# Attention and feed-forward kernel: order and form of the first transfers, z spread by TensorE products, scales of values and M from squares

## The chip, the cores and the metric

The kernel runs on one core of a Trainium2 chip. The metric is the device time of one execution in microseconds (us). A core has five engines that run their own instruction streams side by side: TensorE (PE: matrix products, results in PSUM), VectorE (DVE), ScalarE (ACT: functions and copies), GpSimd (POOL) and SyncE (SP, which here only issues transfers). Each takes its instructions strictly in order, and semaphores make one wait for another. 16 DMA engines move data. TensorE runs at one of two levels of its clock, 1.2 or 2.4 GHz; the profile shows the granted share.

## The reference

Four batches of 8 heads, 576 rows, head size 64. The heads' outputs are laid side by side and become 2304 rows of 512 for a two-layer network.

```python
scores = np.where(causal, -1e9, q @ k.T / sqrt(D));  a = softmax(scores)   # rows + 1e-9
local = a @ v
q_p = phi(q)                                   # phi(x) = x + 1 for x > 0, else exp(x)
mem_out = (q_p @ M_prev) / (q_p @ z_prev + 1e-6)
x = sigmoid(beta) * mem_out + (1 - sigmoid(beta)) * local     # -> 2304 x 512
h = x @ w_in                                   # 512 x 2048
g = np.maximum(h, 0) + alpha * np.minimum(h, 0)
out = g @ w_out                                # 2048 x 512
```

w_in and w_out lie in memory as 64-bit numbers; the kernel makes 32-bit numbers of them by integer operations on VectorE.

## The kernel before

**Stages.** The first 64 rows of all four batches (256 rows, called Z in the code) are done first, with `load_first`, `first_scores` and `first_values`. The remaining 512 rows of each batch follow, in units of a head, with scores, probabilities and values on TensorE, and each 256 rows that are ready go through the network (`moe_in`, `moe_out`) in steps of 256 columns of w_in. The network runs twice over the rows, once for each half of the 2048 columns. The first groups take the weights of the first half as 32-bit numbers; later groups take them as two 16-bit parts in three products.

**Weights.** A piece of w_in is 128x1024 numbers in two transfers of 512 KB (its two column halves). `load_w` loads it, `conv_w` makes 32-bit numbers by three VectorE operations on 128x1024 (`to_f32`) and lets ScalarE square it with a running sum, which gives the weights' scale. `split_w` makes the 16-bit parts. Four pieces form w_in's first half.

**Scales.** Values and M go into one matrix beside each other and need a power of two as scale. Before, VectorE finds their largest magnitude: `prep_vZ` (first rows, two reduces of 128x1024), `prep_v0` (batch 0, three reduces) and `prep_v` (batches 1 to 3, one of 128x2048 and one of 128x512 each). `powers` and `exponents` turn it into a power of two through a transpose and a product on TensorE. The scale stands ahead of the probabilities: their products with it on VectorE must be done before TensorE can transpose them and form the values.

**Other names.** `ones` is the operand of the warm-up products that TensorE does at the start (WARM, 66 before); R is the store of the weights, part of which holds first rows' data at the start; stv and mw hold the largest magnitudes, mv those of batch 0; P the probabilities, PT their transposes, s scores in PSUM, h and y the network's results in PSUM, x the rows that enter the network, gg the activated h; kn, q, vn, zb, E are loads' buffers.

**Order.** Every operation is first recorded by the class `Work`, then issued in the order of the table PLACES, which holds a place for each operation of each phase (so nearly every instruction has the same line in the profile, L827). The order on each engine, SP's included, is thus fixed by that table. It was found by a search with the prices in `price`. All loads of the kernel are issued by SP in one queue:

```python
at = [next(places[op[7]]) for op in self.ops]
for i in sorted(range(len(at)), key=at.__getitem__):
    _, fn, a, kw = self.ops[i][:4]
    fn(*a, **kw)
```

## Time and profile before

| | |
|---|---|
| runs | 544.98, 545.71, 549.67 us, median 545.71 |
| the profiled execution | 547.0 us |
| its span in the profile | 545.2 us |
| TensorE / VectorE / ScalarE / GpSimd busy | 96% / 83% / 69% / 12% |
| chain that ended last | PE 68%, DVE 17%, DMA 7%, ACT 3% |
| granted clock, mean | 0.99 |

An engine is busy when it executes an instruction; the share is an average over stages. The span runs from the first to the last instruction that the profile shows. The windows give busy time in stretches of the span, and the chain of waits follows back, from the last instruction, what released each step.

### The profile page before, as it was taken

The page shows a single profiled execution, that of the slowest core. Times are in us where ns is not written, and L with a number is a line of the kernel's source. Part 1 is how long each engine was busy: PE and PEld are TensorE (multiplying, and loading weights), DVE is VectorE, ACT ScalarE, POOL GpSimd, SP SyncE. Part 2 cuts the span into 40 slices and gives each one's busy share as a digit, 9 for nine tenths or more (in the row PEclk, how much of TensorE's full clock was granted, in tenths as well). Part 3 has the DMA queues.
Part 4 walks back from the last instruction along what each step waited for, and adds up shares of the span by engine and source line. Part 5 has one row for each costly group of instructions (what it writes and reads, how often), then busy time and mean ns, then how long its engine had stood idle before and what let it go on. Part 6 is the DMA issues. An engine that isn't in the chain of part 4 may idle for free.

```text
span 545.2 us, 11977 instructions
## 1 busy us (share of the span) xinstructions
PE 525.1 (96%) x4421; PEld 352.8 (65%) x4421; DVE 451.3 (83%) x1197; ACT 376.4 (69%) x790; POOL 65.1 (12%) x142
## 2 busy tenths in 40 slices
PE   8849999999998999999999999999999999999997
PEld 3537655756676666668576666667676667676663
DVE  5999999999999999999989999978798866533231
ACT  1659888688987578888779788786776755422322
POOL 3000420001110011111112111021211110000000
PEclk9969999999999999999999999999999999999999
DMA  8999968763599989669999826787725534401101
GB/s 289 216 336 205 266 173 226 214 128 95 135 157 185 222 211 176 143 149 179 208 205 229 187 60 129 165 185 160 135 50 112 107 88 117 88 21 49 38 1 38
DMA packets 226026, 82.84 MB, mean 152 GB/s; under 512 B 216224, under 2 KB 216240, under 8 KB 225968
## 3 DMA queue, kind: packets, MB, share of 16 engines
q1 hardware_dynamic: 225968, 82.09, 67.4%
q8 instruction: 34, 0.56, 0.4%
q14 instruction: 24, 0.20, 0.1%
HBM read 35.66 MB, written 5.77 MB: 76 GB/s over the span
## 4 chain that ended last, share of the span: by engine, by line
PE 68%; DVE 17%; DMA 7%; ACT 3%; issue 3%; SPq 2%; POOL 0%; DVEq 0%; ACTq 0%; POOLq 0%
PE h L827 28%; PE y L827 27%; PE s L827 6%; PE bank L827 5%; DMA PT<-P 3%; DVE R L827 3%; DVE E L827 2%; DVE P L827 2%; DVE gg L827 2%; DMA E<-in_moe_w_in_dram 2%; SPq L827 2%; DVE r L827 1%; ACT P L827 1%; DMA R<-in_M_prev_dram 1%; DMA R<-in_moe_w_in_dram 1%
## 5 line engine op out<-in xcount | busy, mean ns | idle before, releaser
L827 PE MATMUL y<-R,gg 128*128 128x512 f16 (+1 forms) x832 | 274.7, 397 | 0.0
L827 PE MATMUL h<-x,R 128*128 128x256 f16 x1536 | 267.3, 273 | 0.2
L827 PEld LDWEIGHTS <-R 128*128 128x128 f16 x1536 | 142.2, 98 | 47.5 <-issue 1.9
L827 PE MATMUL bank<-v,PT 128*128 128x64 f16 x1224 | 146.8, 193 | 3.2 <-DMA PT<-P 3.1
L827 PEld LDWEIGHTS <-PT 128*128 128x128 f16 x1224 | 97.7, 98 | 33.4 <-DMA PT<-P 4.1
L827 PEld LDWEIGHTS <-gg 128*128 128x128 f16 x768 | 73.5, 98 | 39.4 <-DVE gg L827 0.6
L827 ACT ACTIVATE E<-E,mx 128x192 f32<-128x192 f32 (+3 forms) x136 | 81.1, 600 | 25.6 <-DVE mx L827 22.1
L827 POOL TENSOR_SCALAR E<-q,nrm,sm 128x64 f32<-128x64 f32 x112 | 50.5, 463 | 337.2 <-DVE sm L827 263.3
L827 ACT ACTIVATE P<-E,mx 128x640 f16<-128x640 f32 (+3 forms) x112 | 71.8, 673 | 20.0 <-POOL E L827 10.1
L827 DVE SCALAR_TENSOR_TENSOR P<-E,mx,P 128x384 f16<-128x384 f32 (+3 forms) x112 | 76.2, 699 | 7.4 <-ACT P L827 6.0
L827 DVE SCALAR_TENSOR_TENSOR r<-r,oma,h 128x256 f32<-128x256 f32 x128 | 57.5, 475 | 24.2 <-ACT r L827 24.0
L827 ACT ACTIVATE r<-h 128x512 f32<-128x512 f32 x72 | 42.2, 589 | 32.7 <-PE h L827 28.2
L827 DVE SCALAR_TENSOR_TENSOR gg<-r,gsc,gg 128x512 f16<-128x512 f32 x56 | 41.8, 748 | 25.6 <-ACT gg L827 15.2
L827 DVE CUSTOM_DVE_ANT_0 E<-s,mask,pm 128x576 f32<-128x576 f32 (+3 forms) x96 | 57.3, 612 | 4.6 <-PE s L827 3.0
L827 ACT ACTIVATE gg<-r,gsc 128x512 f16<-128x512 f32 x56 | 40.0, 715 | 30.1 <-PE y L827 22.9
L827 PE MATMUL s<-k,qT 128*128 128x64 f16 (+5 forms) x136 | 36.4, 290 | 0.2 <-DVE mx L827 0.2
L827 PE MATMUL s<-k,qS 128*128 128x192 f16 (+4 forms) x120 | 34.8, 294 | 0.0
L827 PE MATMUL h<-R 128*128 128x256 f32 x128 | 32.1, 386 | 0.1
L827 PEld LDWEIGHTS h<-R 128*128 128x128 f32 x128 | 22.7, 190 | 5.6 <-issue 2.1
L827 ACT ACTIVATE xn<-bank,xsc 128x256 f16<-128x256 f32 x28 | 13.1, 469 | 15.3 <-PE bank L827 15.0
L827 ACT ACTIVATION_READ_ACCUMULATOR E<-E,mx 128x1 f32 x124 | 23.3, 188 | 0.0
L827 DVE SCALAR_TENSOR_TENSOR R<-R,wsc 128x1024 f16<-128x1024 f32 x16 | 20.5, 1280 | 0.1
(183 smaller groups left out, 618.1 us busy)
## 6 DMA issues: line engine op xcount, KB each, us to landing
q<-in_q_dram SPq DMA_DIRECT2D x16, 256.0 KB, 5.3
vn<-in_v_dram SPq DMA_DIRECT2D x16, 256.0 KB, 5.1
out_dram<-t SPq DMA_DIRECT2D x16, 256.0 KB, 2.4
kn<-in_moe_w_in_dram SPq DMA_DIRECT2D x6, 512.0 KB, 7.6
kn<-in_moe_w_out_dram SPq DMA_DIRECT2D x6, 512.0 KB, 5.8
kn<-in_k_dram SPq DMA_DIRECT2D x12, 256.0 KB, 3.8
qS<-qT SPq DMA_DIRECT2D x24, 128.0 KB, 2.7
R<-in_moe_w_in_dram SPq DMA_DIRECT2D x4, 512.0 KB, 5.7
```

The lines of the kernel that those rows point to most:

```text
L827: fn(*a, **kw)
```

## The change

**Transfers.** The first rows' loads now come ahead of most of the weights: of the four w_in pieces only the first column half is loaded and made into 32-bit numbers at first (`load_w` and `conv_w` with `cs=(0,)`), the second halves follow. The conversion of these four pieces is in operations of 128x512 in place of 128x1024. Values and M of the first rows come in four transfers of 64x16x64 in place of eight of 64x8x64. alpha, beta and z are issued by ScalarE, not SP.

**z.** z of the first rows, needed on 64 partitions for each batch, was loaded four times with the row repeated. Now four rows are loaded once (4x512), and two TensorE products with a 0/1 matrix spread them over the partitions; ScalarE copies the result from PSUM.

**Scales.** The reduces of `prep_vZ`, `prep_v0` and `prep_v` are gone. ScalarE squares the values (times 2^-10) and sums along each row, and the scale's exponent is taken from the largest of these sums, halved; constants are adapted (SQ, GS, 2^13).

**TensorE at the start.** Warm-up products go from 66 to 40, and two products of 128x256 follow on each of the four converted first halves (PACE) whose results nobody reads.

**Places.** Phases are finer (a name for each head, piece or step), the planner's prices are new, and PLACES is found anew.

```diff
-WARM = 16, 50
+WARM = 16, 24
+PACE = 2
...
     def load_first():
-        for b in range(B):
-            load(*zload(zb[ps, t], b), "Lz")
+        zr = R[12][0:B, 0:H * D]
+        A.dma_start(out=zr, in_=z_prev.rearrange("b h d -> b (h d)"))
...
-        for b in range(B):
-            vv = nat[Z]["v"][b // 2][:, b % 2]
-            Y.dma_start(out=vv[64:128], in_=v[b, :, 0:64, :].rearrange("h p d -> p h d"))
-            Y.dma_start(out=vv[0:64], in_=M_prev[b].rearrange("h d e -> d h e"))
+        for t in range(2):
+            for ps, src in ((slice(64, 128), v[2 * t:2 * t + 2, :, 0:64, :]), (slice(0, 64), M_prev[2 * t:2 * t + 2])):
+                Y.dma_start(out=nat[Z]["v"][t][ps].rearrange("p b h d -> p (b h) d"), in_=src.rearrange("b h p d -> p (b h) d"))
...
     def conv_w(s, cs=(0, 1)):
+        for c in (0, 512) if len(cs) == 1 or not WC[s] else (0,):
+            n = 512 if len(cs) == 1 or not WC[s] else 1024
...
+        if s < 4 and not cs[0]:
+            for i in range(PACE):
+                T.matmul(h0[:, 0], lhsT=r[:, 0:128], rhs=r[:, 0:256], start=True, stop=True)
...
     def prep_vZ():
         for i in range(2):
-            V.tensor_reduce(mv[:, i:i + 1], vn[i].rearrange("p t h d -> p (t h d)"), **ab)
+            A.activation(R[0], vn[i].rearrange("p t h d -> p (t h d)"), AF.Square, scale=2.0 ** -SQ, accum_out=mv[:, i:i + 1])
...
     def prep_v(b):
-        V.tensor_reduce(sv, vn[:, :, 1:NS].rearrange("p h i d -> p h (i d)"), **dict(ab, axis=AX.XY))
-        V.tensor_reduce(mv[:, 0:1], vn[:, :, 0], **dict(ab, axis=AX.XY))
+        A.activation(p["q16"][:, 0:2048].rearrange("p (h c) -> p h c", h=H), vn[:, :, 1:NS].rearrange("p h i d -> p h (i d)"),
+                     AF.Square, scale=2.0 ** -SQ, accum_out=sv)
+        A.activation(p["q16"][:, 0:512].rearrange("p (h c) -> p h c", h=H), vn[:, :, 0], AF.Square, scale=2.0 ** -SQ,
+                     accum_out=mv[:, 0:1])
...
+    zs = R[12][0:B, 512:768]
+    A.copy(zs.rearrange("p (b n) -> p b n", b=B), ident[0:B, 0:B][:, :, None].to_broadcast([B, B, 64]))
+    for t in range(2):
+        pt = psp.tile([128, 512], F32, tag="y", bufs=2)
+        T.matmul(pt, lhsT=zs[:, 128 * t:128 * t + 128], rhs=R[12][0:B, 0:H * D], start=True, stop=True)
+        A.copy(nat[Z]["z"][t].rearrange("p h d -> p (h d)"), pt)
...
     def weights(i):
-        load_w(8 * i)
-        for s in range(8 * i, 8 * i + 8):
+        if i == 0:
+            for f in (load_w, conv_w):
+                for c in range(2):
+                    for s in range(4):
+                        f(s, (c,))
+            w_scale(0)
+        first = 8 * i if i else 4
+        load_w(first)
+        for s in range(first, 8 * i + 8):
```

SP's queue before, from its first load of k on (64x8x64 is a first-row load of one batch; by here all eight w_in halves and q are issued):

```order
L827 DMA R<-in_k_dram 64x8x64 x3
L827 DMA q_1_94<-in_z_prev_dram 64x512
L827 DMA R<-in_k_dram 64x8x64
L827 DMA R<-in_v_dram 64x8x64 x2
L827 DMA R<-in_M_prev_dram 64x8x64 x2
L827 DMA R<-in_v_dram 64x8x64
L827 DMA R<-in_M_prev_dram 64x8x64
L827 DMA R<-in_v_dram 64x8x64
L827 DMA R<-in_M_prev_dram 64x8x64
L827 DMA q_2_95<-in_q_dram 128x8x64 x2
```

And SP's queue now, from its first instruction on:

```order
L1740 DMA R<-in_moe_w_in_dram 128x1024
L1740 DMA R<-in_k_dram 64x8x64
L1740 DMA q_0_93<-in_q_dram 64x8x64 x4
L1740 DMA R<-in_moe_w_in_dram 128x1024
L1740 DMA R<-in_k_dram 64x8x64 x2
L1740 DMA R<-in_M_prev_dram 64x16x64
L1740 DMA kn_90<-in_moe_w_in_dram 128x1024
L1740 DMA R<-in_k_dram 64x8x64
L1740 DMA R<-in_v_dram 64x16x64
L1740 DMA R<-in_M_prev_dram 64x16x64
L1740 DMA E_0_92<-in_moe_w_in_dram 128x1024
L1740 DMA R<-in_v_dram 64x16x64
```

The last first-row load is now behind four w_in halves (128x1024 of 32-bit words each) in place of eight, and no load of z stands among them.

VectorE's piece before at which the first rows' values and M are reduced, behind the maxima of the scores (ISA rows), up to the start of the scale:

```order
L827 TENSOR_REDUCE stv_137<-R 128x1 x2
L827 ISA P_100,zmx_134<-s_0_68,mz 128x64
L827 ISA zmx_134 128x1
L827 TENSOR_TENSOR stv_137<-stv_137 128x1
L827 TENSOR_REDUCE stq_85<-q_2_95 128x1
L827 SCALAR_TENSOR_TENSOR tt_142<-tt_142,str_129 128x2
L827 TENSOR_REDUCE mw_0_139<-bank_67 1x2
```

The same place now:

```order
L1740 TENSOR_TENSOR stv_137<-stv_137 128x1
L1740 ISA P_100,zmx_134<-s_0_68,mz 128x64
L1740 ISA zmx_134 128x1
L1740 TENSOR_REDUCE mw_0_139<-bank_67 1x2
L1740 TENSOR_SCALAR tt_142<-tt_142 128x2
```

And ScalarE's piece that now holds the two Squares, between copies of the first rows' transposed k and the exponentials of their scores (P):

```order
L1740 COPY k_1_102<-y_123 128x512
L1740 COPY q_1_94<-y_124 128x512
L1740 COPY q_0_91<-y_124 64x512 x2
L1740 ACTIVATE R,stv_137<-R 128x1024
L1740 COPY q_0_91<-y_124 64x512 x2
L1740 ACTIVATE P_99,zsm_135<-P_99,zmx_133 128x64 x7
L1740 ACTIVATE R,stv_137<-R 128x1024
```

The two reduces have left VectorE; the Squares stand in ScalarE's order, the second behind seven exponentials.

## Rows read from the trace of the kernel before

**Rows 1.** The page: span, each engine's busy time, and DMA shares in 40 slices:

```profile
span 545.2 us, 11977 instructions
...
PE 525.1 (96%) x4421; PEld 352.8 (65%) x4421; DVE 451.3 (83%) x1197; ACT 376.4 (69%) x790; POOL 65.1 (12%) x142
...
DMA  8999968763599989669999826787725534401101
```

**Rows 2.** Windows (us): length, busy of PE, PEld, DVE, ACT, POOL (instructions), clock, DMA share, GB/s:

```profile
30.00:40.00 10.00, 5.43 (x25) 4.42 (x27) 9.92 (x35) 4.33 (x18) 0.00 (x0) 0.54 0.99 372
40.00:60.00 20.00, 19.00 (x156) 14.66 (x155) 20.00 (x59) 17.76 (x40) 0.48 (x2) 0.97 1.02 242
...
120.00:140.00 20.00, 19.93 (x154) 12.46 (x153) 19.94 (x58) 17.90 (x27) 2.02 (x4) 1.00 0.61 151
140.00:160.00 20.00, 20.00 (x205) 13.12 (x202) 19.86 (x54) 18.30 (x36) 3.36 (x8) 1.00 0.66 122
160.00:180.00 20.00, 18.14 (x191) 13.57 (x188) 18.76 (x37) 15.06 (x26) 0.00 (x0) 1.00 1.07 181
360.00:380.00 20.00, 20.00 (x196) 14.33 (x195) 14.84 (x40) 15.77 (x34) 2.73 (x7) 1.00 0.75 174
```

**Rows 3.** Chain of waits, 0 to 60 us: start, length, what:

```profile
23.11 5.50 DMA R<-in_M_prev_dram
...
29.94 1.21 DVE stv L827
...
36.08 1.97 PE h L827 x8
38.05 1.81 PE y L827 x8
```

**Rows 4.** Timeline of PE: start, length, operation [idle before, releaser]:

```profile
31.42 0.37 PE L827 MATMUL bank<-ident,stv 128*1 128x128 f32 x1 [4.86 <-DVE stv L827]
...
43.53 0.70 PE L827 MATMUL h<-R 128*128 128x256 f32 x2
```

**Rows 5.** Timeline of DVE, 0 to 62 us:

```profile
6.37 0.69 DVE L827 TENSOR_SCALAR R<-R 128x1024 int32<-128x1024 int32 x1 [5.27 <-DMA R<-in_moe_w_in_dram]
...
28.81 2.35 DVE L827 TENSOR_REDUCE stv<-R 128x1 f32<-128x1024 f32 x2 [0.74 <-DMA R<-in_M_prev_dram]
...
37.15 0.69 DVE L827 TENSOR_TENSOR P<-P,zsm 128x512 f32<-128x512 f32 x1
...
49.86 1.80 DVE L827 TENSOR_REDUCE mv<-vn 128x1 f32<-128x1024 f32 x2
...
60.65 0.70 DVE L827 TENSOR_SCALAR R<-q 128x1024 int32<-128x1024 int32 x1 [0.15 <-DMA q<-in_moe_w_in_dram]
```

**Rows 6.** Lines by shape, DVE: count, busy us, mean ns, idle before:

```profile
L827 DVE SCALAR_TENSOR_TENSOR R<-kn,R 128x1024 int32<-128x1024 int32 x10 | 12.0, 1204 | 0.0
...
L827 DVE TENSOR_REDUCE st<-vn 128x1 f32<-128x2048 f32 x3 | 6.8, 2276 | 0.0
...
L827 DVE SCALAR_TENSOR_TENSOR R<-kn,R 128x512 int32<-128x512 int32 x4 | 2.7, 683 | 0.0
...
L827 DVE TENSOR_REDUCE stv<-vn 128x1 f32<-128x512 f32 x3 | 2.0, 681 | 0.0
```

**Rows 7.** Lines by shape, ACT:

```profile
L827 ACT ACTIVATE q<-kn 128x2560 f16<-128x2560 f32 x3 | 7.0, 2326 | 0.0
L827 ACT ACTIVATE kn<-R 128x1024 f32<-128x1024 f32 x6 | 6.3, 1054 | 0.7 <-DVE R L827 0.7
...
L827 ACT ACTIVATION_READ_ACCUMULATOR kn<-R 128x1 f32 x6 | 1.1, 190 | 0.0
```

**Rows 8.** Lines by shape, PE:

```profile
L827 PE MATMUL h<-R 128*128 128x256 f32 x128 | 32.1, 386 | 0.1
L827 PE MATMUL y<-R,gg 128*128 128x512 f32 x64 | 31.5, 606 | 0.0
```

**Rows 9.** Timeline of SP's queue, 0 to 30 us:

```profile
24.46 0.63 SPq L827 DMA_DIRECT2D R<-in_M_prev_dram  x1
```

More of the change, by code (lines that the diff above doesn't have):

```diff
@@ new lines @@
+    "oZ1": (
+        "234 236 250 252 253 254 255 256 257 258 259 260 261 291 292 293 294 296 297 304 308 309 310 311 312 313 314 "
+        "315 316 317"
+    ),
+    "LW00": (
+        "12"
+    ),
+    "LW01": (
+        "71"
+    ),
+    "LW02": (
+        "80"
+    ),
+    "LW03": (
+        "189"
+    ),
+    "LX00": (
+        "270"
+    ),
+    "LX01": (
+        "300"
+    ),
+    "LX02": (
+        "238"
+    ),
+    "LX03": (
+        "276"
+    ),
+    "C00": (
+        "44 52 53"
+    ),
@@ new lines @@
+    "n0": (
+        "203 206"
+    ),
+    "C01": (
+        "72 73 89"
+    ),
+    "n1": (
+        "207 212"
+    ),
+    "C02": (
+        "99 100 106"
+    ),
+    "n2": (
+        "225 226"
+    ),
+    "C03": (
+        "190 192 193"
+    ),
+    "n3": (
+        "227 228"
+    ),
+    "D00": (
+        "271 273 283"
+    ),
+    "c0": (
+        "371 398 399 407 421 459 481 482 623"
+    ),
+    "D01": (
+        "301 345 372"
+    ),
+    "D02": (
+        "269 274 289"
+    ),
+    "D03": (
+        "277 287 290"
+    ),
@@ L90 @@
+    "LW10": (
+        "401 400"
+    ),
+    "LW11": (
+        "404 444"
+    ),
+    "C10": (
+        "402 403 433"
+    ),
+    "c1": (
+        "434 449 471 463 478 486 508 557 577 730 646 709"
+    ),
+    "LW12": (
+        "465 466"
+    ),
+    "C11": (
+        "445 447 448"
+    ),
+    "LW13": (
+        "457 456"
+    ),
+    "C12": (
+        "467 469 470"
+    ),
+    "C13": (
+        "458 461 462"
     ),
     "L0q": (
-        "421 238 250"
+        "338 239 267"
     ),
     "L0k": (
-        "345 360 376 187"
+        "335 337 336 15"
@@ new lines @@
+    "c2": (
+        "686 741 757 805 807 810 831 836 1091"
+    ),
+    "LW22": (
+        "687 660"
+    ),
+    "C21": (
+        "647 700 701"
+    ),
+    "LW23": (
+        "742 702"
+    ),
+    "C22": (
+        "743 744 754"
+    ),
+    "LW30": (
+        "758 755"
+    ),
+    "C23": (
+        "777 782 785"
+    ),
+    "S20": (
+        "837 845"
+    ),
+    "S21": (
+        "852 853"
+    ),
+    "S22": (
+        "854 867"
+    ),
+    "S23": (
+        "868 903"
+    ),
+    "LW31": (
+        "806 786"
+    ),
@@ new lines @@
+    "C30": (
+        "813 830 839"
+    ),
+    "c3": (
+        "843 860 928 1005 1006 1030 1090 1099 1100 1165 1102 1135 1224 1174 1303 1226"
+    ),
+    "LW32": (
+        "846 840"
+    ),
+    "C31": (
+        "844 851 855"
+    ),
+    "LW33": (
+        "943 944"
+    ),
+    "C32": (
+        "878 902 926 879 901 925"
+    ),
+    "C33": (
+        "945 966 1000"
+    ),
+    "S30": (
+        "1118 1133"
+    ),
+    "S31": (
+        "1160 1162"
+    ),
+    "S32": (
+        "1176 1177"
+    ),
@@ L203 @@
+    "S33": (
+        "1220 1222"
+    ),
+    "S00": (
+        "1329 1330"
+    ),
+    "S01": (
+        "1380 1548"
+    ),
+    "S02": (
+        "1565 1588"
+    ),
+    "S03": (
+        "1591 1673"
+    ),
+    "S10": (
+        "1677 1692"
+    ),
+    "S11": (
+        "1699 1710"
+    ),
+    "S12": (
+        "1833 1834"
+    ),
+    "S13": (
+        "1851 1937"
     ),
     "L1q": (
-        "557 681 683 659 1144"
+        "641 483 545 544 1141"
     ),
     "L1k": (
-        "1014 887 1006 889 888 906"
+        "1146 1147 1142 1149 1148 1098"
@@ L1059, with load_w @@
     staging = [[kn, q16] * 4, staging * 2]
-    def load_w(s):
-        work.phase = f"LW{s // 4}"
+    def load_w(s, cs=(0, 1)):
+        work.phase = f"LW{s // 4}{s % 4}" if s > 3 or not cs[0] else f"LX0{s}"
         hf, kind, u = s // 8, s // 4 % 2, s % 4
         st = pieces[s] = staging[s < 8][s % 8]
-        for c in range(2):
+        for c in cs:
             if kind == 0:
@@ L1481, in turned @@
     def turned(i0):
-        work.phase = "BK0" if i0 else "bk0"
+        ph = work.phase = "BK0" if i0 else "bk0"
         n, p = nat[0], pre[0]
@@ L1487, in turned @@
                              i0 + 1 if i0 else 0, 2 if i0 else 3)):
+            work.phase = ph + ("0" if t == "qT" else "1")
             y = p["qT" if t == "qT" else "kT"] = stack[t].rearrange("p (a c) -> p a c", a=NP)
```

1365 lines of the change are left out of this document (1171 added, 194 removed), and 352 rows, old and new, of the table PLACES.

## The prediction

> **What bounds the kernel now.** I read the page first: TensorE (PE) is busy 525.1 of 545.2 us, VectorE (DVE) 451.3, and the row of DMA shares stands at eight tenths or more through most of the first eighth of the span [rows 1]. So at most some 20 us of idle PE can be won, unless work goes. The windows show where it is: 4.57 in 30 to 40 alone, then little, 1.00 in 40 to 60 and none or nearly none in most windows behind it. DVE is as full there: 20.00 in 40 to 60, 19.86 in 140 to 160. Only from 360 on does DVE fall to 14.84 [rows 2]. Two engines run side by side at their limit, and a lead of one is worth only as much as the other can follow.
>
> The chain of waits tells what the start waits for: a load of M (the memory matrices) issued at 23.11 lands 5.50 us later, DVE then reduces values and M to their largest magnitude, and the transposes of the first rows' probabilities start only at 36.08 [rows 3]. PE has a gap of 4.86 us there, and the first real product of the first layer is at 43.53 [rows 4]. PE's granted clock is 0.54 in 30 to 40, a mix of the full and the half level (2.4 and 1.2 GHz), after that gap [rows 2].
>
> **The change, part by part.** *Transfers.* Up to and with the load at 23.11, SP has asked for eight w_in halves of 512 KB and 18 first-row loads of 128 KB, 6,400 KB, landed at 28.61; from SP's first issue at 0.7 that is 229 KB per us [rows 3]. The last first-row load now has ahead of it, itself included, four halves (2,048 KB), eight q and k loads (1,024), four loads of v and M of 256 (1,024), and 8 KB of z: 4,104 KB, 17.9 us at this rate, so 18.6 instead of 28.6. SP's own issue is no limit: one 128 KB load takes it 0.63 [rows 9], eight of these, four of at most twice that and four halves below that make 13 us at most. The new 64x16x64 load has no row; as dear as two old ones or as one, its bytes decide.
>
> *First product.* Once values and M are there, one Square with its accumulator (1.05 + 0.19 [rows 7]) stands where two reduces of 2.35 stood [rows 5]. From the end of the reduce in the chain (29.94 + 1.21) to the transposes at 36.08 were 4.9 us [rows 3]: 18.6 + 1.2 + 4.9 = 24.7 by this chain. DVE's own work is the other bound: from 6.37 to the end of the last probability product at 37.84 it had 31.5 us, of which 0.74 idle ahead of the reduces, 12.4 for whole w_in pieces (four of 0.69 + 2 x 1.20), 2.35 for the reduces and 2 for batch 0 (three operations of 0.68 or 0.69) [rows 5, 6]. That leaves 14.0; the first halves add 4 x (2 x 0.68 + 0.35) = 6.9 (the first step at half of 0.69; at worst 0.69, 1.4 us more). 20.9 us from about 5 on give 25.9 if DVE never waits. I take 27, as both chains hand work to each other. From 36.08 to 43.53 were 7.4 us, with 3.8 of transposes at half clock [rows 3]; at the full level 1.9 less. So the first product comes at 27 + 5.5 = 32.5, by both bounds between 30.5 and 35: PE gains 8.5 to 13 us, I take 9, at the low end, because PE now has eight extra products of 0.39 (PACE) in the same place, and two for z of 0.61 [rows 8], which wait for conversions in PE's order.
>
> *What the extra and missing PE work costs:* 26 fewer warm-ups and these ten products, about 4.3 us, stand ahead of the first product, in time in which PE waits; nothing on the path. If PE did not wait there, the ten would cost their 4.3.
>
> *DVE.* It loses the reduces of the first rows (2.35), of batch 0 (1.80 and a later one of 128x1024, 1.2 by the chain) and of three batches (2.28 + 0.68 each, 8.9 in all) [rows 3, 5, 6]. It gains 12 instructions by halving four pieces: two of 0.683 for one of 1.204, so 0.16 in each of eight, and at most 0.3 in each of four: 0.8 in round figures, 2.5 at worst. By the time batch 1 is built, between 120 and 170 us, it has lost 2.35 + 1.80 + 2.96 - 0.8 = 6.3 (the later reduce of batch 0 left aside); it starts 1.2 earlier, as a half is enough to begin; but between its conversions it now waits for first rows at the start, which I put at 3 us more than before. 6.3 + 1.2 - 3 = 4.5 us of lead, against PE's 9. Since neither has idle time to give up between 40 and 160, PE must wait for about the difference, there or in 160 to 180, where it already had 1.86 idle [rows 2].
>
> *ScalarE (ACT)* takes the magnitudes over: five Squares of at most 1.05 + 0.19 at the start and in batch 0, and per later batch one of 128x2048 (2.33 for 128x2560, so about 1.9; bounds 1.05 and 2.33) and one of 128x512 (0.6 by the same scale, at most 1.05), with two accumulators 2.9 [rows 7]. Together some 15 us. I cost it at nothing: ACT is busy 18.30 of 20 in its fullest window [rows 2]. If that cover is gone it is the slow rival below. The table of places, searched anew, moves everything else; its worth has no row, and I bound it by zero and by the part of PE's lead that DVE's does not cover, 4.5.
>
> *z.* Four loads of 128 KB become one of 8 KB: 504 KB or 2.2 us of transfer at the above rate. DMA is nearly full through the first five slices (68 us), and DVE at 60.65 waits for a weight piece that only just lands [rows 1, 5]; so through this stretch the data alone give a lead of 2.2, a lower bound on the gain if nothing can be done while DVE waits.
>
> *The clock.* The row shows half speed just behind a 4.86 us gap [rows 2, 4]; I expect no such gap, since the second reduce and the late loads leave the chain. That is worth 1.9, already in PE's lead, not beside it. The Trainium skill, "TensorE: Matmul & The Clock Gate", section "HAM oscillation — how this bites in real kernels", says that a wait between groups of matmuls throttles the engine anew. By that rule a wait in mid-kernel would cost more than its own length, and the time would be 546.8; without it the sum below stands. The trace agrees with the rule at 30 to 40 us.
>
> **The sum.** Profiled run 547.0 (span 545.2 and 1.8 around it), minus DVE's lead of 4.5: 542.5. The runs' median, 545.71, is 1.3 below that run, so 541.2. By the data's bound of 2.2 it is 543.5. DMA's share falls past the fifth slice of the span [rows 1], so DVE can use its lead later: I take 541.8, nearer the first.
>
> **Rivals.** *All of PE's lead stays:* 547.0 - 9 - 1.3 = 536.7. For it speaks that DVE is at 14.84 of 20 past 360, so weight splits and later batches' preparation could be put off; against it that DVE is full for 300 us before. *Nothing stays* (the change brings the first product forward and nothing else): DVE's waits at the start, the data up to 68 us and the transposing loads that come later take 4.5 back: 545.7. For it speaks the wait at 60.65, against it that 12 us of DVE work go for good. *The clock falls once more* past 140 us, behind a wait on DVE of the length of the one at 31: ten us at half level lose 5, so 546.8; against it speaks that PE is busy 19.93 to 20.00 of 20 in three of the windows shown past 120 us [rows 2], and its longest wait is the one at 31 [rows 4]. *ACT binds (slower):* at the build of each of three later batches its Squares, 2.9, stand in its order ahead of copies and exponentials that PE and DVE need; 18.30 + 2.9 is over the 20 of that window [rows 2]. With DVE's lead unused, three of them cost 8.7 less the 2.2 of the data: 545.7 + 6.5 = 552.2. It decides once PE loses over 2.6 us to ACT in each batch (7.7 less 2.2 is the 5.5 that make one per cent); against it speaks that ACT has idle time in windows on both sides.
>
> **How the numbers follow.** Forecast 0.42 (own range 540 to 543.5), all kept 0.25, nothing 0.20, clock 0.06, ACT 0.07. A measurement here tells about 1% from no change, 5.5 us. Faster than 540.25: all of the second case and a quarter of the first, 0.36. Slower than 551.2: the ACT case and a little more, 0.08. Same: 0.56. The range 536 to 547 leaves out the ACT case, and about a third of the case in which all is kept.
>
> **What would show it.** In the changed kernel's profile: the last of v and M landing near 18.6; no reduce of 128x1024 before the first product; this product near 34; PE's clock at its full level in 30 to 40; PE waits of some 4 us in all between 60 and 180, ended by DVE; ACT above 18 of 20 in a window without ending PE's waits. Wrong it would be if PE has no more waits than before after 60 us (then about 537), or if these waits are ended by ACT or by transfers.

## The result, and the profile after

The changed kernel takes 548.84 us (median of 20 runs, 546.79 to 550.21), the kernel before on the same chips 545.61 (20 runs): a ratio of 1.0051, 95% interval 1.0034 to 1.0067. Forecast were 541.8 and at most 547.0. The profiled execution took 547.6 us, against 547.0 before: by the two profiles the change costs only 0.6. Ratios compare fast runs alone; of all runs below only e13 had slow ones, two of twelve, at 775 and 1862 us.

The page of the changed kernel, answering [rows 1]:

```profile
span 545.8 us, 11936 instructions
...
PE 527.6 (97%) x4415; PEld 355.1 (65%) x4415; DVE 445.4 (82%) x1195; ACT 389.2 (71%) x815; POOL 66.2 (12%) x142
...
DMA  8999915679578979558999765659235556270101
```

VectorE has 5.9 us less than before, although the reduces that left it took 14.4 us by their durations, and ScalarE 12.8 more. The windows, with the columns of [rows 2]:

```profile
30.00:40.00 10.00, 8.57 (x104) 7.34 (x103) 9.96 (x26) 6.85 (x17) 0.00 (x0) 1.00 1.14 270
40.00:60.00 20.00, 20.00 (x100) 15.39 (x99) 19.33 (x36) 16.56 (x32) 0.00 (x0) 1.00 1.00 311
...
140.00:160.00 20.00, 19.49 (x152) 11.27 (x151) 19.92 (x54) 19.32 (x33) 2.62 (x4) 1.00 0.65 137
160.00:180.00 20.00, 16.80 (x143) 10.87 (x141) 19.95 (x41) 14.60 (x27) 1.50 (x4) 0.91 0.96 195
```

TensorE wins where it was to win: in 30 to 40 it is busy 8.57 instead of 5.43, and the granted clock is 1.00 instead of 0.54. It loses in 160 to 180: 16.80 busy instead of 18.14, and there the clock is 0.91. VectorE is full in both kernels.

PE's timeline at the start (start, length, operation, in brackets the idle time before and what ended it), answering [rows 4]:

```profile
28.14 0.27 PE L1740 MATMUL bank<-ident,stv 128*1 128x128 f32 x1 [0.63 <-DVE stv L1740]
...
32.28 1.07 PE L1740 MATMUL y<-ident,P 128*128 128x128 f32 x8 [1.19 <-DVE P L1740]
...
37.89 4.29 PE L1740 MATMUL h<-R 128*128 128x256 f32 x19
```

The network's first product is at 37.89 instead of 43.53. From there to the end of the span it takes 507.9 us, before 501.7. I call this stretch the rest; below it is worked out in this way for each kernel, from its span and that row. So 5.6 us are won ahead of the first product and 6.2 given back behind it. VectorE and ScalarE at the start, answering [rows 5]:

```profile
6.79 0.17 DVE L1740 TENSOR_SCALAR igc<-igc 128x8 f32<-128x8 f32 x1 [5.68 <-ACT igc L1740]
...
18.69 0.43 DVE L1740 TENSOR_SCALAR R<-kn 128x512 int32<-128x512 int32 x1 [1.52 <-DMA kn<-in_moe_w_in_dram]
```

```profile
26.75 1.06 ACT L1740 ACTIVATE R<-R 128x1024 f32<-128x1024 f32 x1 [1.18 <-DMA R<-in_v_dram]
```

The last of v and M lands at 26.7, not 18.6. PE's idle times from 40 us on add up to 8.06 us, before to 4.12. The longest is this, with the clock in windows behind it:

```profile
163.22 0.83 PE L1740 MATMUL bank<-v,PT 128*128 128x64 f16 x14 [1.83 <-DVE xn L1740]
...
164.29 1.43 PE L1740 MATMUL h<-x,R 128*128 128x256 f16 x5
...
167.30 0.93 PE L1740 MATMUL h<-x,R 128*128 128x256 f16 x7
```

```profile
162.00:164.00 2.00, 0.78 (x15) 0.77 (x15) 2.00 (x6) 1.80 (x4) 0.00 (x0) 0.84 1.23 275
164.00:166.00 2.00, 2.00 (x15) 1.26 (x13) 2.00 (x5) 2.00 (x6) 0.00 (x0) 0.50 0.70 134
166.00:168.00 2.00, 2.00 (x18) 1.67 (x17) 2.00 (x4) 1.43 (x4) 0.00 (x0) 0.81 0.25 48
```

At the half level five products take 1.43 us, at full clock seven take 0.93. Two microseconds at 0.50 and two at 0.81 lose some 1.4 us. Of the 6.2 us, 3.9 are then idle time and 1.4 the clock; about 1 I can't place. Three products that moved behind the first one can be 0.9 of it at most. xn holds the heads' outputs from which x, the network's input, is transposed. What VectorE did ahead of xn:

```profile
159.63 0.74 DVE L1740 SCALAR_TENSOR_TENSOR q<-q,scr,q 128x512 f16<-128x512 f32 x1
160.29 0.68 DVE L1740 TENSOR_TENSOR t<-q,zb 128x512 f32<-128x512 f32 x1
160.90 0.68 DVE L1740 SCALAR_TENSOR_TENSOR q<-q,t 128x512 f32<-128x512 f32 x1
161.50 0.67 DVE L1740 TENSOR_REDUCE nrm<-t 128x8 f32<-128x512 f32 x1
162.09 0.68 DVE L1740 SCALAR_TENSOR_TENSOR gg<-r,gg 128x512 f16<-128x512 f32 x1
162.69 0.47 DVE L1740 SCALAR_TENSOR_TENSOR xn<-bank,xsc,xn 128x256 f16<-128x256 f32 x1
```

xn, which TensorE waits for, stands behind the second batch's preparation. ScalarE's half of it was done at 160.07 (0.46 us from 159.61).

### The profile page after: what moved, and what is told of

Its sections match the earlier page's. It is cut to its first block, busy times and chain, and to the rows that moved or that the text cites. A ratio compares the mean times of both kernels' runs of the same rounds, so it can differ in the third digit from the quotient of the medians.

```text
span 545.8 us, 11936 instructions
## 1 busy us (share of the span) xinstructions
PE 527.6 (97%) x4415; PEld 355.1 (65%) x4415; DVE 445.4 (82%) x1195; ACT 389.2 (71%) x815; POOL 66.2 (12%) x142
## 5 line engine op out<-in xcount | busy, mean ns | idle before, releaser
L1740 PE MATMUL y<-R,gg 128*128 128x512 f16 (+1 forms) x832 | 230.6, 396 | 0.4 <-DVE t L1740 0.3
L1740 PE MATMUL h<-x,R 128*128 128x256 f16 x1536 | 212.8, 274 | 1.2 <-DMA x<-xn 1.2
L1740 POOL TENSOR_SCALAR E<-q,nrm,sm 128x64 f32<-128x64 f32 x112 | 54.7, 501 | 350.4 <-DVE sm L1740 272.9
L1740 ACT ACTIVATE E<-E,mx 128x320 f32<-128x320 f32 (+3 forms) x136 | 80.8, 599 | 22.6 <-DVE mx L1740 20.9
L1740 PE MATMUL bank<-v,PT 128*128 128x64 f16 x1224 | 86.2, 194 | 3.3 <-DVE xn L1740 1.8
L1740 DVE SCALAR_TENSOR_TENSOR P<-E,mx,P 128x640 f16<-128x640 f32 (+3 forms) x112 | 76.2, 699 | 12.2 <-ACT P L1740 11.7
L1740 PEld LDWEIGHTS <-PT 128*128 128x128 f16 x1224 | 67.1, 98 | 21.8 <-issue 2.7
L1740 PE MATMUL s<-k,qT 128*128 128x320 f16 (+5 forms) x136 | 36.6, 290 | 0.2 <-DVE mx L1740 0.2
L1740 PEld LDWEIGHTS h<-R 128*128 128x128 f32 x144 | 26.7, 194 | 4.9 <-issue 1.5
L1740 ACT ACTIVATE t<-y,u 128x512 f32<-128x512 f32 x18 | 12.2, 678 | 11.6 <-PE y L1740 9.0
```

## The experiments

The theories in the expectations: W, the lead is given back because transfers come late or VectorE has too much work; O, the new order has fixed waits of its own past the start, whatever the amount of work; A, ScalarE is filled by the Squares; C, the clock alone; S, SP's queue is a limit of its own. Ratios are to the kernel before on the same chip; first product and rest are in us, from the profiled execution.

| run | median us | ratio (95% interval) | first product | rest |
|---|---|---|---|---|
| before | 545.61 | | 43.53 | 501.7 |
| changed | 548.84 | 1.0051 (1.0034 to 1.0067) | 37.89 | 507.9 |
| e1_w_first | 548.56 | 1.0061 (1.0039 to 1.0083) | 37.88 | 508.1 |
| e5_wide_rows | 547.26 | 1.0007 (0.9987 to 1.0028) | 38.72 | 507.7 |
| e6_conv_first | 547.97 | 1.0026 (1.0008 to 1.0045) | 36.13 | 507.3 |
| e2_old_rest | 567.56 | 1.0413 (1.0386 to 1.0440) | 46.38 | 521.2 |
| e3_reduces | 561.81 | 1.0285 (1.0252 to 1.0319) | 41.44 | 518.6 |
| e4_squares | 557.21 | 1.0219 (1.0193 to 1.0246) | 44.88 | 511.8 |
| e8_short_reduces | 544.59 | 0.9969 (0.9950 to 0.9988) | 44.34 | 498.8 |
| e7_light_conv | 548.91 | 1.0059 (1.0038 to 1.0081) | 41.35 | 508.7 |
| e11_light_late | 549.48 | 1.0068 (1.0045 to 1.0091) | 39.66 | 509.0 |
| e12_moved | 549.57 | 1.0068 (1.0044 to 1.0092) | 36.81 | 508.8 |
| e9_mean_last | 549.04 | 1.0067 (1.0045 to 1.0089) | 37.86 | 508.0 |
| e10_repairs | 551.68 | 1.0106 (1.0086 to 1.0125) | 38.35 | 511.4 |
| e13_light_last | 546.78 | 1.0014 (0.9991 to 1.0037) | 37.42 | 506.7 |
| e15_both_engines | 549.51 | 1.0060 (1.0036 to 1.0084) | 39.48 | 509.5 |
| e14_gpsimd | 549.06 | 1.0047 (1.0022 to 1.0071) | 39.26 | 508.6 |
| e16_q_halves | 548.22 | 1.0044 (1.0031 to 1.0057) | 37.15 | 509.3 |
| e17_all_three | 549.48 | 1.0068 (1.0047 to 1.0089) | 37.90 | 509.7 |
| e18_light_and_q | 546.58 | 1.0009 (0.9994 to 1.0025) | 38.78 | 505.9 |

### The start

*e1, the other three first halves of w_in right behind the first in SP's order:*

```diff
-LW01 71, LW02 80, LW03 189
+LW01, LW02, LW03 behind LW00 (place 12)
```

> The changed kernel with one thing moved: the loads of the first halves of the other three w_in pieces stand right behind the first one, ahead of all first-row loads but none else is changed. Theory W (the first-row loads, in rows of 256 B, take more of the transfer time than their bytes say; the halves behind them land late, VectorE waits some 4 us more at the start than before, and never makes it up): its waits up to 30 us fall from 4.7 to under 2.5, the first product stays within 1.5 us of 37.9, and the time falls by 2 to 4 us, to 545 to 547. Theory O (the new places are worse past the start) and theory A (the Squares fill ScalarE): the early waits fall as well, the time stays within 1 us of the changed kernel's 548.8.

VectorE then waits for no load after q, and ScalarE's Square of v at 26.62 waits for none either. The first product stays:

```profile
12.49 0.69 DVE L694 TENSOR_REDUCE stq<-q 128x1 f32<-128x512 f32 x1 [2.20 <-DMA q<-in_q_dram]
...
37.88 4.29 PE L694 MATMUL h<-R 128*128 128x256 f32 x19
```

The waits on w_in had become waits on q and small loads (4.45, 2.18 and 2.20 us by 12.49), and the work behind them takes as long. In sum VectorE waits 11.5 us by 40, as in the changed kernel (11.3). *e5, the first rows' q, k, v and M read as pieces of 2 KB:*

> The changed kernel with the same bytes for the first rows' q, k, v and M, but read as 64 rows that lie together (2 KB in one piece per partition, and two of them for v and M) in place of 256 B pieces; the data are then others than the reference's, so the first rows' output is wrong, and nothing else changes. Theory W (the 256 B pieces make the first-row loads slow): v's last load lands by 21 us in place of 26.7, the first product comes at 34 us or earlier (37.9), and VectorE's waits before 30 us fall by 3 us or more; the time falls by 2 to 5 us if VectorE's place is what counts. If the pieces' size doesn't matter: landing and time within 1 us of the changed kernel's. Theory O (the new order past the start takes any lead back): the first product comes earlier, the time stays within 1 us of 548.8.

No earlier first product in the profile, although the loads come earlier: SP issues the last one of v at 12.52 instead of 18.63, and the fourth w_in half lands at 21.6 instead of 25.1. But the time moved: the ratio of 1.0007 lies clear below the changed kernel's 1.0051, by about 2.4 us (e6 and e7, on the same chip as e5, have 1.0026 and 1.0059). So the form of the first loads is worth up to some 2 us here; where they are won this one profile, 1.0 above its runs' median, does not show. *e6, VectorE's first conversion ahead of five small operations that wait for beta and alpha:*

```diff
 VectorE's order:
-igc (waits for ScalarE), ..., to_f32 of C00 (places 44, 52, 53)
+to_f32 of C00 (place 30), igc, ...
```

> The changed kernel with VectorE's conversion of the first w_in half moved ahead of five small instructions that wait for beta and alpha. Theory W: the conversion starts at 6.2 in place of 7.6, VectorE gains 0.5 to 1.4 us, and the time falls by no more than that. Theory O: within 0.5 us.

```profile
6.38 0.43 DVE L694 TENSOR_SCALAR R<-R 128x512 int32<-128x512 int32 x1 [5.26 <-DMA R<-in_moe_w_in_dram]
```

```profile
36.13 4.93 PE L694 MATMUL h<-R 128*128 128x256 f32 x22
```

1.8 us earlier, and the rest is the same. But e10, e14 and e17 have the same edit and first products at 38.35, 39.26 and 37.90, so this profile alone does not show a gain. What the first product follows is the sum of VectorE's waits. In the changed kernel and the fourteen made from it that keep its start (e1, e5 to e7 and e9 to e18, the edits of e1, e5 and e6 included) VectorE's waits by 40 us add up to 9.5 to 14.9 us, and the first product's time is this sum and 26.3 to 26.9 us more. In e7, for example, whose start is the changed kernel's to the letter, VectorE waits 3.6 us longer and the first product comes 3.5 us later, with this as the longest wait for a load behind 10 us:

```profile
20.22 0.43 DVE L694 TENSOR_SCALAR R<-kn 128x512 int32<-128x512 int32 x1 [2.09 <-DMA kn<-in_moe_w_in_dram]
```

At the start VectorE's chain is the limit, its work and its waits; the waits differ from one execution to the next, and a single profile can't price a change of the start by less than some 2 us.

### Parts of the change, each with an order not made for it

*e2, the changed kernel up to the first product, then before's order:*

> The changed kernel up to its first product of the network (327 operations, loads among them), and from there on all operations in the relative order of the kernel before. Theory O: the waits of TensorE between 140 and 300 us (7 us in the changed kernel) fall to the 3.3 of before, and the time to 541.5 to 545.5. Theory W: VectorE is no further ahead than before, whatever the order, so waits appear in other places and the time stays within 1.5 us of 548.8. Theory A: ScalarE has the same work, so as W.

*e3, the reduces back on VectorE, the new order kept:*

```diff
-        A.activation(junk..., AF.Square, scale=2.0 ** -SQ, accum_out=mv[:, c:c + 1])
+        V.tensor_reduce(mv[:, c:c + 1], ..., **dict(ab, axis=AX.XY))
```

> The changed kernel, in its own order, with VectorE's reduces for the scales of values and M put back in place of ScalarE's Squares (and their constants). Theory A (ScalarE, with 15 us more, is what holds TensorE): faster than the changed kernel by 2 us or more. Theory W (VectorE paces it): VectorE has 12 us more to do, the first product comes 1 to 3 us later and the time rises by 4 to 11 us, to 553 to 560. If neither paces: within 1.5 us.

*e4, the kernel before with the Squares on ScalarE, its order kept but for 16 of the operations on values, which stand later:*

> The kernel before, in its own order, with the reduces for the scales of values and M replaced by ScalarE's Squares; nothing else of the change. Theory W (VectorE paces the middle): VectorE loses 12 us, and the time falls by 3 to 8 us against the kernel before, to 537.5 to 542.5. Theory A: ScalarE's order gets 15 us of Squares in front of copies and exponentials; no faster than before by more than 1 us, or slower.

All three are slower by 2 to 4 per cent. In e2 two waits show why:

```profile
45.94 0.59 PE L694 MATMUL bank<-wsq,ones 128*128 128x4 f32 x2 [7.79 <-ACT R L694]
...
57.07 0.48 PE L694 MATMUL y<-ident,v 128*128 128x128 f32 x1 [5.82 <-DMA v<-in_k_dram]
```

The old order puts the weights' scale ahead of the first product, and TensorE waits 7.79 us for ScalarE's part in it; and a load that the old order could leave late now stands in the way of an earlier TensorE. Each of the three pairs an order with durations that it was not found for, so none of them prices a part by itself. *e8, the kernel before with the reduces of values and M on 64 columns and nothing on ScalarE* (eleven reduces by the trace; the scales are then those of 64 columns) only takes work away:

> The kernel before with all nine reduces of values and M done on 64 columns per partition: 12 us of VectorE's work left out, nothing put on ScalarE; the scales then come from part of the data. Theory W: VectorE's work is what the Squares were to save, so this is the most the change of engine can give in the old order: the time falls by 2 to 6 us against the kernel before. Theory O (an order found for certain durations suits no others): within 1.5 us of the kernel before, or slower, as with the Squares.

12 us less of VectorE's durations make before 0.3% faster; PE's idle time past 45 us falls from 4.12 to 1.84. That is what the reduces were worth in this order, which was not searched anew.

### What gives the lead back

*e7, the conversion's last two steps on 64 of 1024 columns for the w_out pieces at 45 to 75 us:*

```diff
-V.scalar_tensor_tensor(out=d, in0=lo, scalar=29, in1=d, ...)
+V.scalar_tensor_tensor(out=d[:, 0:n], in0=lo[:, 0:n], scalar=29, in1=d[:, 0:n], ...)   # n = 64 for s 4 to 7
```

> The changed kernel with the second and third step of the conversion of four w_out pieces done on 64 of 1024 columns: 8.5 us of VectorE's work left out around 45 to 75 us, the numbers in w_out are then wrong. Theory W (VectorE has no lead in the middle, so TensorE's is lost): TensorE keeps most of the 6 us that it is ahead at 60 us, its waits on DVE between 140 and 200 us go, and the time falls by 3 to 6 us, to 543 to 546. Theory O: the waits belong to the order and to transfers, the time stays within 1.5 us of 548.8.

```profile
166.57 0.57 PE L694 MATMUL bank<-v,PT 128*128 128x64 f16 x14 [1.83 <-DVE xn L694]
```

The wait keeps its size and its distance from the first product (125.2 us; 125.3 in the changed kernel). VectorE's saved time became its own waits on the way, 9.6 us between 40 and 170 (2.3 in the changed kernel), among them 1.86 for a load at 59.13, 2.38 on ScalarE's E at 62.74 and 1.58 on scores at 66.20. *e11, the same for s 12 to 15, converted at 105 to 131 us:*

> The changed kernel with the second and third step of the conversion (two instructions of 128x1024, 1.21-1.28 us each) shortened to 64 of their 1024 columns for the last four pieces (C30 to C33, converted at 105 to 131 us) instead of the four w_out pieces at 45 to 75 us that an earlier run shortened; the matrices made from these four pieces are then wrong. Some 8 us of VectorE's work go, as much as in that run, in a stretch (91 to 163 us) in which VectorE never waited in the changed kernel, while at 62 to 91 us it waited for TensorE and ScalarE. Theory W, narrowed to the stretch (VectorE, in step with TensorE at 91, works without a wait until 163 and is what TensorE meets there): TensorE's waits at 163, 171.7, 176 and 182.7 (4.1 us) go and with them the granted clock of 0.50 at 164 to 166; the rest from the first product falls from 507.3-508.7 to 502-504.5 us, the time to 543-545.5. Theory O (places in the order, whatever VectorE's amount of work): the waits stay within 0.6 us of their size, the rest at 506.5-508.7, the time at 547.5-549.

```profile
127.51 0.87 DVE L694 SCALAR_TENSOR_TENSOR r<-r,oma,h 128x256 f32<-128x256 f32 x2 [2.07 <-ACT r L694]
```

```profile
166.03 0.57 PE L694 MATMUL bank<-v,PT 128*128 128x64 f16 x14 [0.68 <-DVE xn L694]
...
174.54 0.26 PE L694 MATMUL s<-k,qS 128*128 128x192 f16 x1 [2.17 <-DMA qS<-qT]
```

The first wait shrinks, the one on a copy of q grows from 1.11 to 2.17. *e12, six VectorE operations that nothing needs before 192 us moved from 123 to 152 behind 183 us:*

> The changed kernel with six VectorE instructions that nothing needs before 192 to 314 us put behind the stretch: the third batch's two reduces a2 (stq<-q2, 0.67 us each, at 123.4 and 132.2 us in the changed kernel, first needed at 216) and four small ones of c3 and v0 (0.15 to 0.20 us at 149 to 152) go to places at 185 to 195 us; nothing else changes and the whole computation is kept. 2.0 us of VectorE's work leave the stretch ahead of 163 us. Theory W, narrowed to 91 to 163 us: TensorE's 1.83 us wait at 163 goes almost whole, the clock's fall at 164 with it, the waits at 171 to 183 shrink; the rest falls from 507.3-508.7 to 503.5-506 us, the time to 544.5-546.5. Theory O: the wait at 163 moves or stays, rest 506.5 or more. If the six come in the way at 185 to 195 us, a wait of 1-2 us shows there instead.

The wait stays at 1.82. The two longer ones, 0.67 each, were made up for by waits of 0.16 to 0.44 us within 16 us. *e9, xn ahead of four operations of the second batch:*

```diff
 VectorE's order:
-p11 t, p10 q, p11 nrm, h0_110 gg, o033 xn
+o033 xn, p11 t, p10 q, p11 nrm, h0_110 gg
```

> The changed kernel with one VectorE instruction put elsewhere: o033's evicted half xn<-bank (128x256, 0.47 us), which in VectorE's order stands behind four instructions for the second batch's rows, goes ahead of these four; nothing else is moved. In the changed kernel TensorE waits 1.83 us there at 163.2 us and the granted clock is 0.50 at 164 to 166. Theory O (the new order past the start has its own waits, each with one eviction, copy or issue that stands too late in its engine's order): the wait at 163 goes, the clock stays full there, and the rest from the first product of the network falls from 507.3-508.7 us to 504.5-506.5, the time from 548.5 to 545.5-547. Theory W (VectorE as a whole is late there and takes back what TensorE gains): the wait moves to the next work of VectorE within 10 us, the rest stays at 507.3 us or more. Theory C (the clock alone): the fall at 164 comes without the wait too; then the rest falls by 1.0-1.8 us only, and the half clock still stands at 162-166.

```profile
164.67 1.04 PE L694 MATMUL h<-x,R 128*128 128x256 f16 x4 [2.54 <-DVE r L694]
```

The wait on xn is gone, a longer one on r is there: ScalarE's half of r stands behind an operation that waits for nrm, and nrm came later. *e10 repairs four more places at once:*

> The run before this one (the eviction xn ahead) with four more places: VectorE's first conversion ahead of five small instructions that wait for ScalarE (as in the run that tried it alone, first product 36.1 us instead of 37.9); the transposing transfer of o137's xn ahead of the one for bk23 (TensorE waits 1.25 us for it at 295.6 in the changed kernel); y4_113's addition t2<-part behind bk11's transfers (1.11 us at 171.7); and y4_103's square on ScalarE behind the evictions of PT (0.45 us twice at 79 and 81). Theory O: each wait goes by itself, the rest falls by the 1.83+0.9 of the first place and a further 1.5 to 3 us, to 502-505 us, and with a first product at 36.1-38 the time is 541-544.5 us, under the kernel before. Theory W: what goes here comes back within 20 us of each place as a wait on VectorE; rest 506.5-508.7, time 547-549. Theory A (ScalarE filled by the squares): waits that ScalarE ends take their place; rest over 506.

It is the slowest of this group: 2.54 us on r and 3.84 on t. *e13, VectorE's work cut in the last stretch, 135 to 163 us* (P's second halves of heads 2 to 7 and the second batch's phi on 64 columns):

```diff
-V.scalar_tensor_tensor(out=P[:, 1, c], ...)
+V.scalar_tensor_tensor(out=P[:, 1, c.start:c.start + 64], ...)   # batch 0, h > 1
```

> The changed kernel with VectorE's work cut between 135 and 163 us, the only stretch before the 1.83 us wait in which no run has shown VectorE waiting: the second half of the weights P of heads 2 to 7 of the four-tile row group of batch 0 (128x512 and 128x640, 0.75 and 0.88 us each, eight of them at 135 to 158 us) and the second batch's phi (two of 0.68 us each for its rows, four at 159 to 163) are computed on 64 columns only; these parts of the result are then wrong. 7 to 8 us of VectorE's durations go from the stretch. Theory W, for this stretch alone (the last 28 us before the wait VectorE has more work than TensorE has time, and earlier lightening was eaten by VectorE's own waits on products): TensorE's waits at 163 to 183 fall from 4.1 us to under 1.5, the clock stays full at 164-166, the rest from the first product falls from 507.3-509.0 to 502-504.5 us, the time to 543-545.5. Theory O (fixed waits between engines in the order, not an amount of work): the rest stays at 506.5 or more.

```profile
161.83 0.61 PE L694 MATMUL h<-x,R 128*128 128x256 f16 x4 [0.56 <-DVE r L694]
169.24 0.26 PE L694 MATMUL s<-k,qS 128*128 128x192 f16 x1 [2.53 <-DMA qS<-qT]
```

Of the cuts of work by themselves in the changed kernel (e7, e11, e13) the only one that moved the time: 0.4% by the two ratios, whose intervals just meet. The wait on xn is gone, so VectorE's work ahead of it made it (it is 1.82 or 1.83 in the changed kernel, e1, e5 to e7, e12 and e16); behind it stands qS, the copy of the transposed q. *e15, order alone on both engines: xn and r ahead on VectorE, r ahead on ScalarE:*

> The changed kernel with order alone changed at one place, on both engines: on VectorE o033's xn and h0_111's two halves r ahead of p10, nrm and gg; on ScalarE h0_111's r ahead of p13's activation. No work is taken away, nothing is given to GpSimd. If the wait at 163 us is one of places in the order of two engines together (theory O), it goes and the rest falls by 2 to 3.5 us to 504-506.5, the time to 545-547. If VectorE's amount of work up to there decides (theory W), the wait comes back as one on the transfer of q (qS, 171.7 us: 1.11 in the changed kernel) or on t at 176, 2 to 3.5 us more of it there, rest 506.5-509.

```profile
164.38 0.61 PE L694 MATMUL h<-x,R 128*128 128x256 f16 x4 [0.48 <-DVE r L694]
170.55 0.24 PE L694 MATMUL s<-k,qT 128*128 128x192 f16 x1 [1.49 <-DVE mx L694]
174.00 0.34 PE L694 MATMUL s<-k,qS 128*128 128x192 f16 x1 [3.10 <-DMA qS<-qT]
```

*e14 also gives phi times z of the second batch to GpSimd and takes e6's place in:*

> The changed kernel, whole computation, with four changes: the second batch's products of phi and z (tensor_tensor 128x512, four of 0.68 us on VectorE at 160 to 170 us) computed on GpSimd; o033's half xn and h0_111's two halves r ahead of p11's sum nrm, p10 and gg on VectorE; h0_111's r on ScalarE ahead of p13's activation (in an earlier run the eviction alone was put ahead, and the wait went to r, since ScalarE stood waiting for nrm); VectorE's first conversion ahead of the five small instructions. Theory W for 135-163 us: the wait at 163 goes and the clock's fall with it, the rest falls from 507.3-509.0 to 503.5-506, the time with a first product at 36-38 to 541.5-544.5 us, under the kernel before. Theory O: a wait of the same size shows within 10 us on the next engine (on GpSimd's t, or on the transposing transfers for bk10), rest 506.5 or more.

3.19 us on qS. An operation of 0.68 us on VectorE took 1.38 there, the mean of four. What holds the copy up is SP's queue in the changed kernel:

```profile
163.61 0.53 SPq L1740 DMA_DIRECT2D qS<-qT  x1
164.23 2.13 SPq L1740 DMA_TRANSPOSE x<-xn  x1
166.46 1.26 SPq L1740 DMA_TRANSPOSE qT<-q  x1
167.81 0.54 SPq L1740 DMA_DIRECT2D t<-part  x1
168.41 0.50 SPq L1740 DMA_DIRECT2D qS<-qT  x1
```

SP issues with no gap of over 0.1 us, and the second half of the copy stands behind three others. *e16, the second half right behind the first:*

```diff
 SP's order:
-qS (first half), x<-xn, qT of bk13, t<-part, qS (second half), ...
+qS (first half), qS (second half), x<-xn, t<-part, ..., qT of bk13
```

> The changed kernel with two places of SP's queue changed and nothing else: the second half of bk10's copy qS<-qT goes right behind the first (in the changed kernel the first issues at 163.61 and the second at 168.41, with the transfer x<-xn, bk13's transposing transfer and t<-part between them), and bk13's transposing transfer (1.26 us at 166.46) behind bk11's copies. Theory S (the run of several transfers that SP issues one after another from 157 to 178 us without a gap is a limit of its own beside VectorE's work): TensorE's wait for qS at 171.7 (1.11 us) goes, the one for xn at 163 (1.83) stays, the rest falls from 507.3-509.0 to 506-507.5, the time to 547-548. Theory O (each repaired place hands its wait to the next): the 1.1 us come back within 15 us, rest 507.3-509.

The wait on qS is gone, but this profile alone does not show that the edit took it away: with SP's order untouched it is 1.11 in the changed kernel, 0.23 and 0.26 in e1 and e7, and none in e6. The wait on xn stays (1.82 at 162.47), and the one on PT<-P at 182.09 takes 1.20 instead of 0.94. *e17, SP, VectorE and ScalarE together:*

> The changed kernel, whole computation, with the order changed on all three engines at the one place: SP as in the run before this; VectorE with o033's xn and h0_111's halves r ahead of p11, p10 and nrm, gg of h0_110 later, s037's second maximum (the one that frees the scores' bank, waited for 1.49 us at 170.6 when only xn and r were moved) ahead of p13; ScalarE with r ahead of p13's activation; and VectorE's first conversion ahead of the five small instructions. Theory S: the waits at 163, 171 and the clock's fall behind them go together, the rest falls from 507.3-509.0 to 503-505.5, the time to 541-545 us with a first product at 36-38. Theory W (VectorE's amount of work up to there): with the same work on VectorE the wait only moves, rest 506.5-509, time 546.5-549.5.

```profile
167.72 0.26 PE L694 MATMUL s<-k,qS 128*128 128x192 f16 x1 [0.86 <-DMA qS<-qT]
172.16 5.28 PE L694 MATMUL y<-R,gg 128*128 128x512 f16 x12 [3.70 <-DVE t L694]
```

*e18, e13 and e16 together:*

> The run that cut VectorE's work between 135 and 163 us (the weights' second halves and the second batch's phi on 64 columns; these parts of the result are wrong) with the two places of SP's queue changed as well. In that run the 1.83 us wait at 163 had gone to 0.56, and a wait of 2.53 us for qS at 169.2 stood in its place, with the granted clock at 0.57 from 170 to 174 behind it; rest 506.7, ratio 1.0014. Theory S (behind VectorE's work stands SP's queue, one limit behind the other): the wait for qS goes and the clock stays full at 168-174; the rest falls from 506.7 to 502.5-504.5, the time to 541-544 us, the ratio to 0.991-0.997. Theory O: the wait for qS turns into another of 2 us or more within 15 us, rest 506 or more.

```profile
170.35 2.75 PE L694 MATMUL y<-R,gg 128*128 128x512 f16 x12 [1.69 <-DVE t L694]
174.65 0.27 PE L694 MATMUL h<-x,R 128*128 128x256 f16 x1 [0.76 <-DMA x<-xn]
181.58 1.75 PE L694 MATMUL bank<-v,PT 128*128 128x64 f16 x54 [1.11 <-DMA PT<-P]
```

Best rest of the family, 2.0 us less than the changed kernel's, and it still waits 4.1 us between 163 and 182; e13's wait of 2.53 us on qS is gone. Theories W and S each describe one layer; none of them alone is the cause. Between 160 and 185 us xn and r on VectorE, mx, the copy of q on SP, the addition t, and the transposing loads all end within a few us of each other, and whichever is taken away uncovers the next. None of the orders tried with the whole computation is faster than the kernel before. No theory met its figures throughout. O's were met in the time or the rest of e1, e7, e12, e13 and e14, W's in those of e6, e9 and e17. The gains that O expected of order alone (e2, e9, e10, e15) did not come: e2, put at 541.5 to 545.5, took 567.6. And e3 and e10 were slower than any theory had said.

## Why the prediction was wrong

**First product: 32.5 forecast, 37.9 measured.** Direction right, size off (the prediction's list of signs has 34 for the same product). The landing at 18.6 took one mean rate for all bytes; the last load of v landed at 26.7, and SP, which was to need 13 us at most, issued it only at 18.63. But e1 shows that this landing was not the term that decided: with w_in's halves early, no load is waited for past 12.5 us, and the first product does not move. (By e5 the form of the loads is still worth up to some 2 us of the time.) The term that failed is in VectorE's bound, 20.9 us of work "from about 5 on", raised to 27 for mutual waits. The last probability product ends at 33.3: VectorE started its conversions at 7.6 instead of 5 and waited 11.2 us by 40 (before 7.4). The work came out nearly as summed, 33.3 less these waits being 22.1; the waits, put at some 6, were mis-sized. TensorE's lead was 5.6 us, not 9.

**VectorE's lead: 4.5 forecast, none measured. This is the step that failed.** Counting what is left to do, with one duration for each shape, VectorE had 283.0 us left at 160 us before and 283.3 after; TensorE had 376.9 and 372.7. The reduces that left ahead of the second batch, 6.3 us net of the splits, did not put VectorE ahead. The count is even kind to the change: the 283.0 hold 5.9 us of reduces for the last two batches, which the forecast's 4.5 left out. In the work that both kernels do VectorE was some 4 to 6 us behind at 160 (the two figures come from two ways to take a shape's duration), and some 4 behind at 40 already, so the start lost it. Its splits cost 2.0 us by its durations instead of 0.8; where it was to start 1.2 earlier and to wait 3 more, it began converting 1.2 later and waited 3.8 more by 40. The reduces that the kernel before did between 40 and 160 us won nothing back: 2.3 us of waits between 30 and 100 (before 0.2) were not in the sum at all, and where the remainder went stays open.

**"TensorE must wait for about the difference, there or in 160 to 180".** Right in place. The sign named for it, some 4 us of waits between 60 and 180 ended by VectorE, came out at 5.2 us, of which VectorE ended 2.6, ScalarE 1.5 and transfers 1.1. TensorE's lead by the same count is 4.2 us at 160, 1.2 at 180 and -0.2 at 200. With VectorE's lead at nothing or less, the same step gives back all of it, which was the rival at 545.7 ("nothing stays"). But the mechanism was named too simply. VectorE alone does not pace that place: e13 took 7 to 8 us of its work away in the last 28 us and the rest fell by 1.2 us, since SP's queue and ScalarE's order stand behind it. And work taken away earlier (e7, e11) brought nothing, since VectorE then waited for other engines and loads, 9.6 us between 40 and 170 in e7.

**Past nothing: the 3 us that were lost.** Two things were not in the sum. The clock rival was held at 0.06 with ten us at half level; it came in small, 1.4 us behind a wait of 1.83. The rule of the Trainium skill, "TensorE: Matmul & The Clock Gate", section "HAM oscillation — how this bites in real kernels", that a wait between groups of matmuls throttles the engine anew, is told there of longer waits than this one; the traces agree with it behind the waits of 3.10 to 3.84 us in e15, e14, e17 and e10, each with 0.50 behind it. Shorter waits differ: 0.50 behind the 1.83 here, 1.00 behind 2.17 in e11 (172 to 178 us), and 1.00 in 160 to 180 [rows 2] around this wait of the kernel before:

```profile
167.54 0.20 PE L827 MATMUL bank<-v,PT 128*128 128x64 f16 x1 [1.78 <-DMA PT<-P]
```

And the new order has waits that the old one lacked, such as four on ScalarE's PT between 79 and 91 us (1.5 us in all) and 1.25 on x<-xn at 295.6. "Its worth has no row", the prediction says of the new table, and bounds it by zero and 4.5. These waits speak for a worth below zero, but no run shows it apart from the other changes: e2, the one with the old order behind the start, was slower still.

**The run of the profile and the runs timed.** The profile of after shows 0.6 us more than that of before, the medians 3.2. That of before lies 1.4 over its median, that of after 1.2 under its own. The four kernels with after's order past the start (changed, e1, e5, e6) have rests of 507.3 to 508.1, so after's 507.9 is not short. Nine kernels share its start (changed, e7, e9, e11 to e13, e15, e16, e18), and their first products lie at 36.8 to 41.35, 38.5 in the mean, against 37.89. With a rest of 507.8 and the 1.8 around the span a mean start gives 548.1: part of the 1.2 is then an early start in the profiled execution, by VectorE's waits there; the other 0.7 stays open.

**ScalarE** was costed at nothing. It is above 18 of 20 in several windows, as foretold, and ended 1.5 us of PE's waits. No run isolates it, since e4's order was not made for it. What z and the fewer warm-up products brought was not tried alone either. The full clock in 30 to 40 us came as forecast.

## What to carry to other kernels

When two engines are full side by side, a lead at the start is worth what the slower of them keeps, and its lead has to be counted by work left at a time, not by instructions removed. Where the order is fixed by hand or by a search, look at the place where a stage ends and the next begins: if several engines and a queue are all due there, repairing one wait can give it to the next. Here only the runs that took work away in the last stretch (e13, e18) shortened what stands behind the first product. A new order can carry a price of its own, of either sign.

## What the runs showed of the hardware

After waits of 3 to 4 us the granted clock stayed at half for longer than the wait. Windows of e17, behind its 3.70 us:

```profile
172.00:174.00 2.00, 1.84 (x5) 0.69 (x5) 2.00 (x5) 1.56 (x3) 0.40 (x2) 0.50 1.09 207
174.00:176.00 2.00, 2.00 (x7) 0.63 (x5) 1.96 (x5) 2.00 (x3) 0.00 (x0) 0.50 0.93 191
176.00:178.00 2.00, 2.00 (x8) 0.96 (x7) 2.00 (x3) 0.73 (x2) 0.00 (x0) 0.50 0.96 253
```

Six microseconds at 0.50 cost about 3, nearly as much as the wait. Another surprise is how little small VectorE operations weigh. In e12 four of 0.15 to 0.20 us (0.69 by their durations) left the last 14 us ahead of xn, and xn came only 0.12 us earlier, counted from the first product. In the changed kernel the next operation starts 0.07 to 0.13 us behind the start of each of the four, 0.39 in sum, so their durations overlap with what follows.
